# Three pairs of maxima tiles beside each imaginary row's chain, and those rows split and summed by ScalarE and GpSimd

## The chip, the cores and the metric

The kernel runs on one core of a Trainium2 chip. The core has five engines that work beside each other, each through its own instructions in order: TensorE (PE in the profile, with its weight loads as PEld), VectorE (DVE), ScalarE (ACT), GpSimd (POOL) and SyncE (SP), which here issues nearly all DMA transfers. PSUM, into which PE writes, has eight banks of 128 x 512 float32. GpSimd doesn't touch PSUM in this kernel. The metric is the time of one execution on the device in microseconds.

## The reference

Two mixers run on the same `x` (2048 x 512, float32) and are blended by a gate per row:

```python
g = _sigmoid((x * gate_w).sum(-1, keepdims=True))
a = x @ dft_hid_re.T ;  b = x @ dft_hid_im.T          # Fourier mixing along the hidden dimension
A = dft_seq_re @ a - dft_seq_im @ b                    # and along the sequence, real part
q, k, v = heads of x @ wqkv                            # 32 heads of 16
B = concat(softmax(q @ k.T / 4) @ v) @ wo
out = g * A + (1 - g) * B
```

(These lines are shortened from the reference; shapes are written out in it.) The weights of the attention are large (drawn x 64), so the softmax needs its row maxima, and float32 accuracy is kept by splitting operands.

## The kernel before, in words

**Split operands.** Where full accuracy is needed, a float32 tile is written as a high part (a cast to `float32r`) and a low part (the tile minus the high part). `hi_lo` (L73) does it: the cast on ScalarE, the subtraction on VectorE or on the engine that it is given. A product is then three matmuls (`mm3`, L77: high x high, high x low, low x high). A chain of four such triples over the hidden dimension, twelve matmuls, makes one 128 x 512 row tile.

**The order of the work.** The order on every engine is that of the program text (`manual_schedule`). It has these stages:

1. Projections to q and k (L156 to L172), stored split in DRAM (`qk_d`).
2. Value rows (L255 to L264): for each of 16 row tiles `s` a chain into a psS bank, copied to `vt` by ScalarE and VectorE.
3. Imaginary rows (L276 to L297): for each of 16 row tiles a chain with the imaginary part of the hidden matrix into a psS bank; the result is split into `bt` (`hi_lo`, L284) and stored to `b_d` by SP. In the same turn of the loop the row's product with the gate's weight is summed into a column of `z` (L289), the `xa` row for two turns later is loaded, and, for `s` = 2 to 5, a part of the output weight `wo` is split (cast on ScalarE, subtraction on GpSimd) and stored; its next part is loaded only after that store. For `s` = 6 to 9 a part of the real hidden matrix (`wre`) is split in the same way (`split(1)`). The pool of `bt` and `wt` tiles, `hl`, has two buffers; raw loads have six.
4. The main stage (from L768): the gate's values from `z` (`gate`, L603), then the real rows (`real`, L343, copied out of PSUM by ScalarE as `y` and split by GpSimd), the transform along the sequence (`dft`, L368) and the attention, interleaved on PE by written-out patterns (L705 to L707). The stage opens with six bursts of six real-row matmuls, with scores and maxima tiles between them (L771 to L783).

**Maxima tiles.** The softmax's row maxima come from tiles of their own: `a_tile` (L197) multiplies 48 rows of `qs` and `ks` for one head of a pair into one PSUM bank, and VectorE reduces the bank to one column of `mx`. The tiles of a pair's two heads use different row halves of PE. Each head has 1024 such tiles, and some are done ahead, in `visit` (L243), between the chains of stages 2 and 3: two per head and visit, from the value row 10 on, until `LEAD` = 44 per head are done: 22 visits. When the first 32 per head are there, `m_rows` (L213) transposes the block's maxima and SP writes them into `qs`.

**PSUM.** Three psS banks (`s`: rows and scores), three psA banks (`a`), one psD bank (`d`) and one bank `acc`, which collects the attention's values in the main stage. A visit's four tiles go to the three psA banks and the psD bank.

The lines the change touches most are these:

```python
        hi_lo(bt[:, 0], bt[:, 1], ps)
        nc.sync.dma_start(b_d[s], bt.bitcast(F32))
        if s + 2 < NT:
            xgs[s + 2] = staged(xa[s + 2])
        xg = xgs.pop(s)
        nc.vector.scalar_tensor_tensor(xg, xg, 1.0, gwb, op0=ALU.mult, op1=ALU.mult, accum_out=z[:, s:s + 1])
```

Of the kernel before, what the change touches and what calls it, by code (L numbers as in the profile page):

```python
# [9 lines left out]
F32 = mybir.dt.float32  # L10
F32R = mybir.dt.float32r
AF = mybir.ActivationFunctionType
ALU = mybir.AluOpType
AX = mybir.AxisListType

P = 128
S = 2048
D = 512
# [3 lines left out]
KT = D // P  # L22
NT = S // P
UNITS = NP * 32
LEAD = 44
RAW = 6
PSUM = bass.MemoryType.PSUM
DRAM = bass.MemoryType.DRAM
# [3 lines left out]
def mix_kernel(ctx: ExitStack, tc: tile.TileContext, xa_t, xa, wqkv, w_hid, w_seq, wo, gate_w, out):  # L32
# [5 lines left out]
    nc = tc.nc  # L38
    ctx.enter_context(tc.manual_schedule())

    psS = ctx.enter_context(tc.tile_pool(name="psS", bufs=3, space=PSUM))
    psA = ctx.enter_context(tc.tile_pool(name="psA", bufs=3, space=PSUM))
    psO = ctx.enter_context(tc.tile_pool(name="psO", bufs=1, space=PSUM))
    psD = ctx.enter_context(tc.tile_pool(name="psD", bufs=1, space=PSUM))
# [17 lines left out]
    z = const.tile([P, NT], F32, name="z")  # L62
# [8 lines left out]
    acc = psO.tile([P, 512], F32, name="acc")  # L71

    def hi_lo(hi, lo, src, lo_eng=None):  # L73
        nc.scalar.copy(hi, src)  # L74
        (lo_eng or nc.vector).tensor_tensor(lo, src, hi.bitcast(F32), ALU.subtract)  # L75

    def mm3(ps, sh, sl, mh, ml, first, last):  # L77
        nc.tensor.matmul(ps, sh, mh, start=first, stop=False)  # L78
        nc.tensor.matmul(ps, sh, ml, start=False, stop=False)  # L79
        nc.tensor.matmul(ps, sl, mh, start=False, stop=last)  # L80

    right = tc.tile_pool(name="st1", bufs=1, side="right", reuse_waits="tile")
    st1 = right.__enter__()
# [4 lines left out]
    gwb = st1.tile([P, D], F32, name="gwb")  # L88
# [3 lines left out]
    def staged(src):  # L92
        raw = st1.tile([P, D], F32, name="raw", bufs=RAW)
        nc.sync.dma_start(raw, src)
        return raw
# [9 lines left out]
    def split(n):  # L105

        for _ in range(n):
            load_ahead()
            if loaded:
                hi, lo, raw, lo_eng, shape = loaded.pop(0)  # L110
                hi_lo(hi, lo, raw.rearrange("p (s t) -> p s t", s=4) if shape else raw, lo_eng)
            load_ahead()
# [7 lines left out]
    def bank():  # L120
        nonlocal banks
        banks += 1
        return (psS if banks % 2 else psA).tile([P, 512], F32, name="s" if banks % 2 else "a")


    with tc.tile_pool(name="qk", bufs=1, reuse_waits="tile") as pool:
# [29 lines left out]
        for tb in range(4):  # L156
            for c in range(2):
# [9 lines left out]
                for ct in range(4):  # L167
                    ps = bank()
# [28 lines left out]
    def a_tile(i, h, ps=None):  # L197
        p, j = divmod(i, 64)
        qt, kb = divmod(j, 4)
        if ps is None:  # L200
            ps = psA.tile([P, 512], F32, name="a")
        r = slice(64 * h, 64 * h + 48)
        nc.tensor.matmul(ps, qs[p % 2][r, qt * P:(qt + 1) * P], ks[p % 2][r, kb * 512:(kb + 1) * 512],  # L203
                         start=True, stop=True)
        user = nc.vector.tensor_reduce(mx[p % 2][:, h, qt, kb:kb + 1], ps, AX.X, ALU.max)  # L205
        hf = j // 32
        a_left[p, hf] = a_left.get((p, hf), 64) - 1
        if not a_left[p, hf]:
            nc.vector.tensor_reduce(nm[hf], mx[p % 2][:, :, 8 * hf:8 * hf + 8, :], AX.X, ALU.max, negate=True)
            deferred.append((p, hf))  # L210
        return user
# [14 lines left out]
    def run_deferred():  # L226
        while deferred:
            m_rows(*deferred.pop(0))
# [12 lines left out]
    a_next = 0  # L241

    def visit(i):  # L243

        nonlocal a_next
        if i < 10 or a_next == LEAD:
            return
        if a_next % 32 >= 4:
            run_deferred()
        for j in range(2):  # L250
            for h in range(2):
                a_tile(a_next, h, psD.tile([P, 512], F32, name="d") if j and h else None)
            a_next += 1

    for s in range(NT):  # L255
        t = xab[s // 4][:, s % 4]
        ps = psS.tile([P, 512], F32, name="s")
        for kt in range(KT):
            r = slice(kt * P, (kt + 1) * P)
            mm3(ps, t[:, 0, r], t[:, 1, r], wv[0][kt], wv[1][kt], kt == 0, kt == KT - 1)  # L260
        visit(s)
        pv = ps.rearrange("p (r h d) -> p r h d", h=2, d=DH)
        nc.scalar.copy(vt[:, s, :, 0:16], pv[:, :, 0])
        nc.vector.tensor_copy(vt[:, s, :, 17:33], pv[:, :, 1])  # L264
# [11 lines left out]
    for s in range(NT):  # L276
        t = ab[s]
        ps = psS.tile([P, 512], F32, name="s")
        for kt in range(KT):
            r = slice(kt * P, (kt + 1) * P)  # L280
            mm3(ps, t[:, 0, r], t[:, 1, r], wch[:, kt], wcl[:, kt], kt == 0, kt == KT - 1)
        visit(NT + s)
        bt = st1.tile([P, 2, D], F32R, name="hl", bufs=2)
        hi_lo(bt[:, 0], bt[:, 1], ps)  # L284
        nc.sync.dma_start(b_d[s], bt.bitcast(F32))
        if s + 2 < NT:
            xgs[s + 2] = staged(xa[s + 2])
        xg = xgs.pop(s)
        nc.vector.scalar_tensor_tensor(xg, xg, 1.0, gwb, op0=ALU.mult, op1=ALU.mult, accum_out=z[:, s:s + 1])  # L289
        if 2 <= s < 2 + KT:  # L290
            wt = st1.tile([P, 2, D], F32R, name="hl", bufs=2)
            hi_lo(wt[:, 0], wt[:, 1], wos.pop(0), nc.gpsimd)
            nc.sync.dma_start(wo_d[s - 2], wt.bitcast(F32))
            if s + 1 < 2 + KT:
                wos.append(staged(wo[:, s - 1]))
        elif s >= 2 + KT:
            split(1)  # L297
    run_deferred()
    assert a_next == LEAD
    right.__exit__(None, None, None)  # L300
# [547 lines left out]
```

## Time and profile before

| what | value |
|---|---|
| median of 3 runs | 1778.67 us (1777.91 to 1779.57) |
| profiled execution | 1778.45 us, its span 1776.3 us |
| PE / VectorE / ScalarE / GpSimd busy | 98% / 78% / 64% / 19% of the span |
| 128 x 512 maximum out of PSUM, VectorE | 682 ns |
| 128 x 512 copy out of PSUM, ScalarE (`y`) | 581 ns |
| 128 x 512 subtraction, GpSimd / VectorE (`hl`) | 1283 / 687 ns |
| value rows | 95 to 144 us |
| imaginary rows | 144 to 216 us |

In the profile, a group of instructions is written as line, engine, operation, written tile `<-` read tile; then the busy time, the mean duration of one in ns, and the engine's idle time just before them with what ended it. In the timeline the first two numbers are the start and the length in us of a run of equal instructions (`x3`: three of them), and the bracket has the wait before it. Slices are fortieths of the span, their digits tenths of busy time; PEclk is the clock that PE was granted, in tenths of full speed.

### The profile page before, as it was taken

The page shows a single profiled execution, that of the slowest core. Times are in us where ns is not written, and L with a number is a line of the kernel's source. Part 1 is how long each engine was busy: PE and PEld are TensorE (multiplying, and loading weights), DVE is VectorE, ACT ScalarE, POOL GpSimd, SP SyncE. Part 2 cuts the span into 40 slices and gives each one's busy share as a digit, 9 for nine tenths or more (in the row PEclk, how much of TensorE's full clock was granted, in tenths as well). Part 3 has the DMA queues.
Part 4 walks back from the last instruction along what each step waited for, and adds up shares of the span by engine and source line. Part 5 has one row for each costly group of instructions (what it writes and reads, how often), then busy time and mean ns, then how long its engine had stood idle before and what let it go on. Part 6 is the DMA issues. An engine that isn't in the chain of part 4 may idle for free.

```text
span 1776.3 us, 32641 instructions
## 1 busy us (share of the span) xinstructions
PE 1747.2 (98%) x12753; PEld 1044.3 (59%) x12753; DVE 1392.9 (78%) x2347; ACT 1144.5 (64%) x2242; POOL 342.8 (19%) x353
## 2 busy tenths in 40 slices
PE   8999899999999999999999999999999999999997
PEld 7876554456665665665656655665665666544443
DVE  5228878888888888888888888888888888899943
ACT  5211267777677676776776666666666676677775
POOL 0111121221222232221221232221222222100011
PEclk9999899999999999999999999999999999999998
DMA  8754610314132242414146434313142535460113
GB/s 283 238 108 159 216 24 7 55 31 73 43 67 61 58 108 83 90 37 78 43 78 243 92 99 105 80 51 72 48 79 67 122 90 96 156 157 22 38 28 123
DMA packets 77994, 164.71 MB, mean 93 GB/s; under 512 B 14592, under 2 KB 15616, under 8 KB 74000
## 3 DMA queue, kind: packets, MB, share of 16 engines
q1 hardware_dynamic: 77584, 162.56, 36.0%
q8 instruction: 100, 1.64, 0.4%
q14 instruction: 54, 0.44, 0.1%
q0 software_dynamic: 256, 0.07, 0.0%
HBM read 107.47 MB, written 54.52 MB: 91 GB/s over the span
## 4 chain that ended last, share of the span: by engine, by line
PE 89%; DVE 6%; ACT 2%; DMA 1%; issue 1%; DVEq 0%; SPq 0%; ACTq 0%
PE d L339 33%; PE acc L630 25%; PE a L203 11%; PE s L621 11%; DVE mx L205 5%; PE s L78 2%; PE s L79 2%; PE s L80 2%; ACT pt L622 1%; PE a L79 1%; PE a L80 1%; PE a L78 1%; DVE y L396 1%; DMA b<-hl 1%; PE a L339 0%
## 5 line engine op out<-in xcount | busy, mean ns | idle before, releaser
L205 DVE TENSOR_REDUCE mx<-a 128x1 f32<-128x512 f32 x2026 | 1248.1, 682 | 237.7 <-PE a L203 221.3
L622 ACT ACTIVATE pt<-s 128x512 f32<-128x512 f32 x2008 | 1026.1, 622 | 424.5 <-PE s L621 360.1
L203 PE MATMUL a<-ks,qs 48*128 48x512 f32 x2026 | 817.1, 420 | 4.2 <-DVE mx L205 2.4
L621 PE MATMUL s<-qs,ks 50*128 50x512 f32 x2008 | 769.9, 413 | 0.4 <-ACT pt L622 0.2
L339 PE MATMUL d<-xab,ch 64*128 64x512 f32 x2016 | 649.0, 396 | 3.6 <-DVE mx L205 3.6
L630 PE MATMUL acc<-pt,vt 128*17 128x512 f32 x4096 | 506.1, 597 | 0.0
L339 PEld LDWEIGHTS d<-xab,ch 64*128 64x128 f32 x2016 | 365.7, 184 | 128.4 <-DVE mx L205 66.3
L621 PEld LDWEIGHTS s<-qs,ks 50*128 50x128 f32 x2008 | 366.7, 185 | 110.0 <-ACT pt L622 29.8
L203 PEld LDWEIGHTS a<-ks,qs 48*128 48x128 f32 x2026 | 367.0, 185 | 87.6 <-DVE mx L205 58.5
L339 PE MATMUL d<-xab,cl 64*128 64x512 f32 x1008 | 399.7, 396 | 0.0
L323 POOL CAST ch<-craw 128x512 fp32r<-128x512 f32 x126 | 76.9, 611 | 829.7 <-PE d L339 334.1
L339 PEld LDWEIGHTS d<-xab,cl 64*128 64x128 f32 x1008 | 185.5, 184 | 63.7 <-DVE mx L205 47.6
L630 PEld LDWEIGHTS acc<-pt,vt 128*17 128x17 f32 x4096 | 87.8, 96 | 194.0 <-issue 191.2
L324 POOL TENSOR_TENSOR cl<-craw,ch 128x512 fp32r<-128x512 f32 x126 | 162.2, 1288 | 10.1
L339 PE MATMUL d<-wre,xab 64*128 64x512 f32 (+1 forms) x348 | 96.5, 410 | 5.0 <-ACT pt L622 2.5
L339 PEld LDWEIGHTS d<-wre,xab 64*128 64x128 f32 (+1 forms) x348 | 60.7, 187 | 40.2 <-issue 23.5
L339 PE MATMUL d<-wo_hl,o_hl 64*128 64x512 f32 (+1 forms) x261 | 70.9, 397 | 0.0
L339 PEld LDWEIGHTS d<-wo_hl,o_hl 64*128 64x128 f32 (+1 forms) x261 | 47.0, 185 | 13.9 <-issue 9.5
L74 ACT CAST hl<-s 128x512 fp32r<-128x512 f32 x32 | 18.7, 585 | 55.6 <-PE s L80 45.0
L75 DVE TENSOR_TENSOR hl<-s,hl 128x512 fp32r<-128x512 f32 x32 | 22.0, 687 | 31.8 <-ACT hl L74 31.8
L356 POOL CAST xab<-y 128x512 fp32r<-128x512 f32 x16 | 9.8, 611 | 164.7 <-ACT y L355 131.7
L634 ACT COPY oe<-acc 128x512 f32<-128x512 f32 x31 | 18.2, 587 | 32.0 <-PE acc L630 32.0
(123 smaller groups left out, 897.1 us busy)
## 6 DMA issues: line engine op xcount, KB each, us to landing
craw<-w_seq SPq DMA_DIRECT2D x128, 256.0 KB
qk<-hl SPq DMA_DIRECT2D x32, 512.0 KB
qs<-qk SPq DMA_DIRECT2D x96, 128.0 KB
ks<-qk SPq DMA_DIRECT2D x96, 128.0 KB
b<-hl SPq DMA_DIRECT2D x16, 512.0 KB
xab<-b SPq DMA_DIRECT2D x16, 512.0 KB
o<-oe SPq DMA_DIRECT2D x62, 128.0 KB
oh<-nh SPq DMA_DIRECT2D x12, 512.0 KB
```

The costliest lines, as they stand in the source:

```text
L75: (lo_eng or nc.vector).tensor_tensor(lo, src, hi.bitcast(F32), ALU.subtract)
L78: nc.tensor.matmul(ps, sh, mh, start=first, stop=False)
L79: nc.tensor.matmul(ps, sh, ml, start=False, stop=False)
L80: nc.tensor.matmul(ps, sl, mh, start=False, stop=last)
L203: nc.tensor.matmul(ps, qs[p % 2][r, qt * P:(qt + 1) * P], ks[p % 2][r, kb * 512:(kb + 1) * 512], start=True, stop=True)
L205: user = nc.vector.tensor_reduce(mx[p % 2][:, h, qt, kb:kb + 1], ps, AX.X, ALU.max)
L323: nc.gpsimd.tensor_copy(h1, raw)
L324: nc.gpsimd.tensor_tensor(l1, raw, h1.bitcast(F32), ALU.subtract)
L339: i = nc.tensor.matmul(self.ps, st[r], mv[r], start=not self.begun, stop=stop)
L621: nc.tensor.matmul(ps, ks[p % 2][rr, kt * P:(kt + 1) * P], qs[p % 2][rr, q0:q0 + 512], start=True, stop=True)
L622: return nc.scalar.activation(pts[u][:, 2 * qb + h], ps, AF.Exp, bias=0.0, scale=DH ** -0.5)
L630: nc.tensor.matmul(acc[32 * j:32 * j + 17], vt[:, kt, p, 16 * h:16 * h + 17], pt[:, j], start=kt == 0, stop=kt == NT - 1)
```

## The change

`visit` does nothing in the value rows any more (`i < NT`). In the imaginary rows, fifteen visits (after the chains 0 to 14) do three tiles per head each, 45 per head in all instead of 44. The two further tiles of a visit go to the bank `acc` and to a psS bank. The imaginary row is copied by ScalarE from PSUM to a new float32 tile `bf` (two buffers), and GpSimd makes both parts of `bt` from it. The gate's product is done by GpSimd, and its sum over the row by ScalarE, as an activation `Copy` with an accumulator. VectorE has neither of them any more.

```diff
-LEAD = 44
+LEAD = 45
...
-        if i < 10 or a_next == LEAD:
+        if i < NT or a_next == LEAD:
             return
         if a_next % 32 >= 4:
             run_deferred()
-        for j in range(2):
+        for j in range(3):
             for h in range(2):
-                a_tile(a_next, h, psD.tile([P, 512], F32, name="d") if j and h else None)
+
+                ps = (None, None, None, psD, acc, psS)[2 * j + h]
+                if ps in (psD, psS):
+                    ps = ps.tile([P, 512], F32, name="d" if ps is psD else "s")
+                a_tile(a_next, h, ps)
             a_next += 1
...
         visit(NT + s)
+
+        bf = st1.tile([P, D], F32, name="bf", bufs=2)
+        nc.scalar.copy(bf, ps)
         bt = st1.tile([P, 2, D], F32R, name="hl", bufs=2)
-        hi_lo(bt[:, 0], bt[:, 1], ps)
+        nc.gpsimd.tensor_copy(bt[:, 0], bf)
+        nc.gpsimd.tensor_tensor(bt[:, 1], bf, bt[:, 0].bitcast(F32), ALU.subtract)
         nc.sync.dma_start(b_d[s], bt.bitcast(F32))
         if s + 2 < NT:
             xgs[s + 2] = staged(xa[s + 2])
         xg = xgs.pop(s)
-        nc.vector.scalar_tensor_tensor(xg, xg, 1.0, gwb, op0=ALU.mult, op1=ALU.mult, accum_out=z[:, s:s + 1])
+        nc.gpsimd.tensor_tensor(xg, xg, gwb, ALU.mult)
+        nc.scalar.activation(xg, xg, AF.Copy, accum_out=z[:, s:s + 1])
```

## The prediction

> **What bounds the kernel now.** I read the page's shares and slices first, then the stretch that the diff touches (0 to 235 us) by timeline, waits and groups. From the page, engines and slices:
>
> ```profile
> PE 1747.2 (98%) x12753; PEld 1044.3 (59%) x12753; DVE 1392.9 (78%) x2347; ACT 1144.5 (64%) x2242; POOL 342.8 (19%) x353
> ...
> PE   8999899999999999999999999999999999999997
> ...
> PEclk9999899999999999999999999999999999999998
> ```
>
> PE is never short of work except at the start, in the fifth slice (178 to 222 us) and at the end. So a change made before 222 us is worth what it moves the point at which the main stage starts to flow. That point is the third burst of six real-row matmuls (L339), which starts at 221.88, just after ScalarE's first copy `y` (L355, 221.24).
>
> The value rows run from 95.0. A chain of twelve matmuls alone takes 2.73 us; with a visit behind it 3.61. The first imaginary-row chain starts at 144.00. Timeline there, VectorE:
>
> ```profile
> 151.18 1.89 DVE L205 TENSOR_REDUCE mx<-a 128x1 f32<-128x512 f32 x3
> 152.98 0.68 DVE L205 TENSOR_REDUCE mx<-d 128x1 f32<-128x512 f32 x1
> 153.58 0.68 DVE L75 TENSOR_TENSOR hl<-s,hl 128x512 fp32r<-128x512 f32 x1
> 154.18 0.68 DVE L289 SCALAR_TENSOR_TENSOR raw<-raw,gwb 128x512 f32<-128x512 f32 x1
> ```
>
> Six operations at a pitch of 0.60 fill the 3.65 us from one visit to the next: VectorE is full, and PE (2.79 + 0.86) just as much. Then ScalarE gets stuck, in the next view (its timeline):
>
> ```profile
> 165.78 0.59 ACT L74 CAST hl<-s 128x512 fp32r<-128x512 f32 x1 [0.92 <-PE a L203]
> 170.35 0.62 ACT L74 CAST hl<-raw 128x512 fp32r<-128x512 f32 x1 [3.98 <-DMA raw<-wo]
> 171.60 0.59 ACT L74 CAST hl<-s 128x512 fp32r<-128x512 f32 x1 [0.64 <-DMA b<-hl]
> 176.52 0.62 ACT L74 CAST hl<-raw 128x512 fp32r<-128x512 f32 x1 [4.33 <-DMA raw<-wo]
> ```
>
> In visits with an output-weight part (s = 2 to 5) the part's load arrives late, the next row's cast stands behind it on ScalarE, VectorE's subtraction behind that, the maxima behind that. Visits take 4.3 to 6.8 us, about 10 us lost. So this stage has two bounds: VectorE's own work, and a loop through ScalarE and DMA. What the new operations will cost is in the groups by shape:
>
> ```profile
> L357 POOL TENSOR_TENSOR xab<-y,xab 128x512 fp32r<-128x512 f32 x16 | 20.5, 1283 | 1.3
> L472 POOL TENSOR_TENSOR no<-no 128x512 f32<-128x512 f32 x12 | 15.4, 1286 | 20.0 <-DMA no<-r 20.0
> ...
> L356 POOL CAST xab<-y 128x512 fp32r<-128x512 f32 x16 | 9.8, 611 | 164.7 <-ACT y L355 131.7 <-PE a L203 33.0
> ```
>
> **The change, part by part.** The profiled execution took 1778.45 us (span 1776.3 and 2.15 around it), 0.2 below the median of the runs shown; the sum is made against 1778.45.
>
> *Six visits leave the value rows:* 6 x (3.61 - 2.73) = -5.3. Nothing else in that stage is longer than 2.73 (ScalarE 0.38, VectorE 0.42 per chain), so the first imaginary chain starts at 138.7.
>
> *A third pair of tiles per visit:* on PE one pair costs 0.235 (tiles at 209.03 and 209.38 are one and a half pairs apart), so a visit's period is 3.65 + 0.23 = 3.88. VectorE: six maxima at 0.60 = 3.6, and nothing else. Both fit in 3.9. The new PSUM places (`acc`, unused until the first values, and a third of psS) cost nothing by themselves, but the visit's last tile now takes the psS buffer of the row chain before, so PE can run about one and a half rows ahead of ScalarE's copy.
>
> *The rows and the gate on ScalarE and GpSimd.* Here I find the new bound. On GpSimd stand, per row, cast, subtraction and product: 0.70 + 1.35 + 1.29 = 3.34 (durations above; pitch 0.70 and 1.35 from the pair at 222, and from two subtractions in 2.64). ScalarE's sum with accumulator waits for that product, and **the next row's copy `bf` is queued behind the sum on ScalarE**; GpSimd's next cast waits for that copy. The two engines run in turn, not beside each other. One turn: sum 0.65, copy 0.59, hand-over 0.06 (221.83 to 221.89), GpSimd 3.34, hand-over 0.06 = **4.70**, above PE's 3.88.
>
> The sum's duration is not in the trace. Lower end 0.52, the pitch of plain activations (two in 1.09); upper end 0.98, an activation with a vector scale, 0.77 (L393), and a short one for the read-out, 0.21 (L605). VectorE's read-out cost 0.08, so I take 0.65, the row nearest to it; over 15 turns the ends are -2 and +5.
>
> For s = 2 to 9 ScalarE also casts a weight part (0.62) after the sum, and GpSimd subtracts it (1.35) ahead of the next cast: 0.65 + 0.62 + 0.07 + 1.35 + 3.34 + 0.06 = **6.09**.
>
> On top come the loads. For s = 2 to 5 the weight loop is: cast 0.62, subtraction 1.36, SP's store and load issues 0.4, landing 3.7 to 4.2 (166.62 to 170.35, 160.06 to 164.24) = 6.1 to 6.6. The store loop of buffer `hl`: landing 4.5 (167.14 to 171.60), cast 0.70, subtraction 1.29 = 6.5. I take 6.4 for four turns; ends 6.1 (hidden) and 7.5 (waits one behind another, as in the 6.8 of now). At s = 6 the four real-part loads are issued behind that row's store and land 4.8 after the subtraction (179.40 to 184.21); the cast could start at 2.1, so 2.7 is added; lower end 0.
>
> GpSimd's two-input operation took 1.75 once, at 157.92, while VectorE did a product of two SBUF operands; the other rows are 1.27 to 1.32. I take 1.29, since the change leaves VectorE only maxima out of PSUM there. At 1.75 thirty operations would add 14. The Trainium skill (GPSIMD Engine Reference, Specifications) says that GpSimd shares its SBUF interface with VectorE and that they collide when VectorE has two SBUF inputs. By that rule nothing collides after the change, so its sum is mine; by the slow row it would be 14 more.
>
> Chain 0 ends at 141.65; its copy, GpSimd's three and the hand-overs put the first sum at 145.75. Then 2 x 4.70 + 4 x 6.4 + (6.09 + 2.7) + 3 x 6.09 + 5 x 4.70 = 85.6, so the sixteenth sum starts at **231.35**. Today the corresponding VectorE sum ends at 216.92.
>
> *The start of the main stage.* ScalarE: sum 0.65, the gate's exponential (0.25), two exponentials at 0.51, then the copy `y` at 233.3 instead of 221.24: **+12.1**. PE will have done both first bursts by then and waits; VectorE's maxima stand behind the gate's small operations (to about 233). Today's wait of 2.44 for a maximum ahead of the first burst goes, but it is late no more. After today's wait the granted clock was 0.50 from 216 to 219.3; the longer wait (some 6 us) puts the same dip on the third burst and what follows: +1.5, half of 3.3 being lost; ends 0 and 3.
>
> *One tile per head less in the main stage:* -0.25, one pair; ends 0 and -0.5. Row maxima for the first block come up at the same count (36), under the slower loop: nothing. SP's stores wait for GpSimd instead of VectorE, the row loads behind them are two rows ahead: nothing while turns last over 4 us, else the load's landing of about 4.
>
> Sum: 1778.45 + 12.1 + 1.5 - 0.25 = **1791.8**, 0.75% slower.
>
> **The rivals.**
>
> *PE sets the pace (faster).* Where: ScalarE between sum and next copy. If the turn took under 3.9, because GpSimd's product or the sum didn't hold the next copy back, the stage would last 16 x 2.79 + 15 x 1.09 = 61.0 from 138.7, and the first burst start at 200 instead of 215.86: 1763. For it: VectorE is full now and would be free, the maxima no longer stand behind the weights' loads. Against it: both engines work in order, and every row of GpSimd is 1.27 or more. It decides at an average turn of 5.71 - 13.3/15 = 4.8.
>
> *The clock falls inside the stage (slower still).* After a wait of 1.17 at 180.63 matmuls of 0.23 pitch ran at 0.43, with 0.50 granted until 188. With turns of 6.1 to 6.4 PE waits about 2 us in each. At half clock a visit takes 5.1 + 1.7 = 6.8, over eight visits some 5 more than the turn, and up to 10 more if it stays so to s = 15: 1797 to 1807. Against: PE is ahead by more than one row, and a PE that has caught up has no waits. The Trainium skill (TensorE: Matmul & The Clock Gate, Why this matters for your kernels) lets the clock fall only after gaps of some 3 us; the row above fell after less, and the measurement decides. By its rule this rival would be nothing; the sum without it stands.
>
> *The late end is hidden (same).* PE still has the real rows' matmuls and could make up for waiting: 1778. Against: they need ScalarE's copy of each row (PE waits 0.45 and 0.50 us for `y` at 221.88 and 226.52 already), and the main stage shows no idle PE in which to catch up.
>
> **How the numbers follow.** Forecast case 0.70 (1784 to 1799: all low ends -2 -1.2 -2.7 -1.5 -0.25 and most of the high ones), PE's pace 0.09, falling clock or slow GpSimd 0.14, hidden 0.07. Range 1782 to 1803: it leaves out the first rival, the hidden end and a part of the second. What a measurement of this kernel tells from no change is about 0.2% (3.6 us). Faster 0.09; same 0.07; slower 0.84.
>
> **What would show it.** First imaginary chain near 138.7. ScalarE rows of the sum with "POOL raw" as releaser, GpSimd's casts released by "ACT bf", in turns of about 4.7 (plain) and 6.1 to 6.5 (s = 2 to 9); GpSimd busy over 70% from 142 to 231. VectorE idle, PE waiting for `bf` in the psS tile of the visits. The gate's exponential near 232. Wrong if turns are under 4.8 on average, if the copy of a row doesn't wait for the sum before it, or if PE is busy throughout.

## The result, and the profile after

The changed kernel takes 1788.22 us (median of 5 runs, 1786.14 to 1789.95), the kernel before 1779.57 us (5 runs, 1777.91 to 1782.27). The ratio over the runs is 1.0046, 95% interval 1.0035 to 1.0057 (the medians alone would give 1.0049): slower by 0.46%, where 0.75% was forecast and 1782 to 1803 us was the range.

The traced execution of the changed kernel took 1789.95 us (span 1788.1), 11.5 us more than the traced one of before (1778.45), while the medians are 8.65 apart: one trace lies at the upper end of its runs, the other near the lower end of its own. Times inside the stage are compared by the traces below, verdicts by the ratios.

The page's shares and slices after:

```profile
PE 1749.0 (98%) x12753; PEld 1047.3 (59%) x12753; DVE 1373.0 (77%) x2299; ACT 1154.2 (65%) x2274; POOL 391.8 (22%) x401
...
PE   8999889999999999999999999999999999999997
...
PEclk9999899999999999999999999999999999999998
```

PE's slices differ by one digit, in the sixth (223 to 268 us). From 300 to 1700 us PE is busy 1393.33 us before and 1393.43 after: the main stage is nearly the same, and the loss is in the imaginary rows. ScalarE's timeline at two plain rows, and at s = 6 and 7:

```profile
145.04 0.63 ACT L298 ACTIVATE raw<-raw 128x512 f32<-128x512 f32 x1 [3.32 <-POOL raw L297]
145.58 0.19 ACT L298 ACTIVATION_READ_ACCUMULATOR raw<-raw 128x1 f32 x1
145.67 0.57 ACT L289 COPY bf<-s 128x512 f32<-128x512 f32 x1
149.56 0.63 ACT L298 ACTIVATE raw<-raw 128x512 f32<-128x512 f32 x1 [3.32 <-POOL raw L297]
...
178.85 0.63 ACT L298 ACTIVATE raw<-raw 128x512 f32<-128x512 f32 x1 [4.07 <-POOL raw L297]
179.38 0.18 ACT L298 ACTIVATION_READ_ACCUMULATOR raw<-raw 128x1 f32 x1
183.28 0.62 ACT L74 CAST wre<-raw 128x512 fp32r<-128x512 f32 x1 [3.71 <-DMA raw<-w_hid]
183.80 0.58 ACT L289 COPY bf<-s 128x512 f32<-128x512 f32 x1
188.41 0.63 ACT L298 ACTIVATE raw<-raw 128x512 f32<-128x512 f32 x1 [4.03 <-POOL raw L297]
```

And GpSimd's between the two plain sums:

```profile
146.30 0.61 POOL L291 CAST hl<-bf 128x512 fp32r<-128x512 f32 x1 [1.29 <-ACT bf L289]
146.99 1.29 POOL L292 TENSOR_TENSOR hl<-bf,hl 128x512 fp32r<-128x512 f32 x1
148.24 1.29 POOL L297 TENSOR_TENSOR raw<-raw,gwb 128x512 f32<-128x512 f32 x1
```

Read in order of time, this is one chain that goes back and forth: sum (145.04), next row's copy (145.67), cast (146.30), subtraction, product, next sum (149.56), 4.52 us from sum to sum. Each engine waits while the other works. The waits of the stretch from 136 to 245 us say the same:

```profile
ACT raw L298 <- POOL raw L297: 59.0, 16, 4.1
POOL hl L291 <- ACT bf L289: 44.9, 8, 35.9
...
ACT bf L289 <- PE s L80: 2.4, 1, 2.4
```

ScalarE waited for the product in all sixteen rows, and for PE's chain once, at the first row. After that PE was never what a copy waited for. At the end of the stage PE stands (its timeline from 219 us):

```profile
219.34 1.53 PE L348 MATMUL d<-wre,xab 128*128 128x512 f32 x6
...
221.46 1.65 PE L348 MATMUL d<-wre,xab 128*128 128x512 f32 x6
225.02 0.49 PE L630 MATMUL s<-qs,ks 50*128 50x512 f32 x1 [1.91 <-ACT bf L289]
229.74 0.79 PE L630 MATMUL s<-qs,ks 50*128 50x512 f32 x1 [4.23 <-ACT pt L631]
...
231.35 2.93 PE L348 MATMUL d<-wre,xab 128*128 128x512 f32 x6
...
235.10 1.65 PE L348 MATMUL d<-wre,xab 128*128 128x512 f32 x6
```

In the kernel before, the third burst reads:

```profile
221.88 1.66 PE L339 MATMUL d<-wre,xab 128*128 128x512 f32 x6
```

So it starts at 231.35 instead of 221.88, and takes 2.93 instead of 1.66. At the fourth burst (224.14 before) the shift is 10.9, and up to 1200 us it stays between 10.7 and 11.1; by 1705 us it has come down to 10.1.

### The profile page after: what moved, and what is told of

The parts are those of the page before. It is cut to its first block, busy times and chain, and to the rows that moved or that the text cites. A ratio compares the mean times of both kernels' runs of the same rounds, so it can differ in the third digit from the quotient of the medians.

```text
span 1788.1 us, 32639 instructions
## 1 busy us (share of the span) xinstructions
PE 1749.0 (98%) x12753; PEld 1047.3 (59%) x12753; DVE 1373.0 (77%) x2299; ACT 1154.2 (65%) x2274; POOL 391.8 (22%) x401
## 4 chain that ended last, share of the span: by engine, by line
PE 87%; DVE 5%; POOL 3%; ACT 2%; issue 1%; DMA 1%; SPq 0%; DVEq 0%; POOLq 0%; ACTq 0%
PE d L348 33%; PE acc L639 25%; PE s L630 11%; PE a L203 11%; DVE mx L205 4%; PE s L79 2%; PE s L78 2%; PE s L80 2%; ACT pt L631 1%; POOL hl L292 1%; POOL raw L297 1%; PE a L79 1%; PE a L80 1%; PE a L78 1%; DMA raw<-wo 1%
## 5 line engine op out<-in xcount | busy, mean ns | idle before, releaser
L205 DVE TENSOR_REDUCE mx<-a 128x1 f32<-128x512 f32 x2003 | 1233.2, 681 | 253.4 <-PE a L203 237.2
L333 POOL TENSOR_TENSOR cl<-craw,ch 128x512 fp32r<-128x512 f32 x126 | 162.2, 1287 | 10.1
L298 ACT ACTIVATE raw<-raw 128x512 f32<-128x512 f32 x16 | 10.1, 631 | 59.0 <-POOL raw L297 59.0
L268 DVE COPY vt<-s 128x256 f32<-128x256 f32 x16 | 6.8, 424 | 36.3 <-ACT vt L267 36.3
```

Of the source, the lines that this page charges most:

```text
L333: nc.gpsimd.tensor_tensor(l1, raw, h1.bitcast(F32), ALU.subtract)
```

## The experiments

**The rows and the gate alone (e1), the visits alone (e2).** e1 is the kernel before with the new lines for rows and gate, e2 the changed kernel with the old ones:

```diff
-        hi_lo(bt[:, 0], bt[:, 1], ps)
+        bf = st1.tile([P, D], F32, name="bf", bufs=2)
+        nc.scalar.copy(bf, ps)
...
+        nc.gpsimd.tensor_copy(bt[:, 0], bf)
+        nc.gpsimd.tensor_tensor(bt[:, 1], bf, bt[:, 0].bitcast(F32), ALU.subtract)
...
-        nc.vector.scalar_tensor_tensor(xg, xg, 1.0, gwb, op0=ALU.mult, op1=ALU.mult, accum_out=z[:, s:s + 1])
+        nc.gpsimd.tensor_tensor(xg, xg, gwb, ALU.mult)
+        nc.scalar.activation(xg, xg, AF.Copy, accum_out=z[:, s:s + 1])
```

That is e1's edit of the kernel before; e2 is the reverse edit of the changed kernel, whose visits stay.

> Before's 22 visits of two tiles per head, with the changed rows and gate (ScalarE copy, GpSimd split and product, ScalarE sum). Theory (the turn of ScalarE and GpSimd sets the stage's pace, 4.51 us plain and 5.8 to 6.4 with a weight part, whatever the visits are): turns as in the changed kernel, but begun at 144.0 instead of 138.1, so 5.9 us slower than the changed kernel: 1794 us, range 1791 to 1797. Rival (the third pair of tiles in each visit, or the PSUM banks it takes, is what holds the stage): at most the time of before, 1779 us.

Measured: 1796.19 us, the kernel before beside it 1781.08; ratio 1.0084 (1.0070 to 1.0097). The turns are the changed kernel's, plain ones at 4.52 (from 151.60 to 156.11 and 160.64), and the third burst starts at 238.34, 7.0 later than in the changed kernel (5.9 was expected; the first sum is 6.6 later, and the turn at s = 6 took 9.90 instead of 9.56). The theory's number holds, the rival's doesn't: without the third pair of tiles the turns are as long, and the stage ends later because it begins later.

> The fifteen visits of three tiles per head, with before's rows and gate (ScalarE cast, VectorE subtraction and gate sum). Theory: no turn of ScalarE and GpSimd; VectorE is the bound with six maxima, subtraction and gate sum, 6 x 0.60 + 0.60 + 0.66 = 4.86 us a visit, and the visits with an output-weight part stay at 6.2 to 6.8: third burst of real rows near 226 instead of 221.9, 1783 us, range 1779 to 1787. Rival (the visits cost nothing, only the moved rows and gate do): 1779 - 5 = 1774 us or less.

Measured: 1781.99 us, ratio 1.0002 (0.9993 to 1.0010): no difference. By its absolute time that lies in the theory's range, by its ratio between theory and rival: the visits neither gain nor lose. The trace shows both halves. The stage begins at 138, as in the changed kernel, but VectorE's plain turns are 4.80 (146.25, 151.04, 155.84), the third burst starts at 228.54 (226 was expected), and ScalarE's lines show the old stall, longer:

```profile
176.69 0.62 ACT L74 CAST hl<-raw 128x512 fp32r<-128x512 f32 x1 [5.90 <-DMA raw<-wo]
177.93 0.59 ACT L74 CAST hl<-s 128x512 fp32r<-128x512 f32 x1 [0.63 <-DMA b<-hl]
186.02 0.62 ACT L74 CAST wre<-raw 128x512 fp32r<-128x512 f32 x1 [7.51 <-DMA raw<-w_hid]
```

So the two halves of the change are +0.84% and 0, and together +0.46%: the visits give the stage an earlier start (5.9 us), which a stage at ScalarE's and GpSimd's pace can use, and one at VectorE's pace spends on the further maxima and the longer stalls.

**The order on ScalarE (e3), and on GpSimd (e5).** In e3 the sum is issued one row late, from a tile of its own:

```diff
         nc.scalar.copy(bf, ps)
+        if s:
+            nc.scalar.activation(pg, pg, AF.Copy, accum_out=z[:, s - 1:s])
...
-        nc.gpsimd.tensor_tensor(xg, xg, gwb, ALU.mult)
-        nc.scalar.activation(xg, xg, AF.Copy, accum_out=z[:, s:s + 1])
+        pg = st1.tile([P, D], F32, name="pg", bufs=2)
+        nc.gpsimd.tensor_tensor(pg, xg, gwb, ALU.mult)
+        if s == NT - 1:
+            nc.scalar.activation(pg, pg, AF.Copy, accum_out=z[:, s:s + 1])
```

> The changed kernel with ScalarE's sum of a row's gate product issued after the copy of the next row (the product goes to a tile of its own). Theory: the next row's copy no longer stands behind the product, plain rows go at PE's 3.9 us, rows with real-part weights at GpSimd's own 4.5, rows with output weights at 6.2 by their loads: 9 us less than the changed kernel, 1779 us, range 1776 to 1783. Rival (the loads and PE's clock set the pace, the order on ScalarE does not): 1788 us, unchanged.

Measured: 1775.93 us, ratio 0.9964 (0.9951 to 0.9978). The same work on the same engines, with the sum one place later, turns a loss of 0.46% into a gain of 0.36%. This is the experiment that decides for the order on ScalarE: the plain copies come at 3.89 and 3.94 (141.57, 145.46, 149.40), PE's pace, and PE's chain is what they wait for:

```profile
145.46 0.59 ACT L289 COPY bf<-s 128x512 f32<-128x512 f32 x1 [3.30 <-PE s L80]
...
149.40 0.59 ACT L289 COPY bf<-s 128x512 f32<-128x512 f32 x1 [2.74 <-PE s L80]
```

The gain is larger than expected: 9 us were forecast, the third burst starts 13.0 earlier than in the changed kernel (218.31), and the time lies just under the range. Behind the late loads at s = 6 the next copy follows after 1.61 us (181.24, 182.85), since PE's row was ready, and the three after it at 4.61, 4.04 and 3.88, where 4.5 was expected.

In e5 the product moves ahead on GpSimd, and the sum stays where it was on ScalarE:

```diff
         nc.scalar.copy(bf, ps)
         bt = st1.tile([P, 2, D], F32R, name="hl", bufs=2)
+        xg = xgs.pop(s)
+        nc.gpsimd.tensor_tensor(xg, xg, gwb, ALU.mult)
+        nc.scalar.activation(xg, xg, AF.Copy, accum_out=z[:, s:s + 1])
         nc.gpsimd.tensor_copy(bt[:, 0], bf)
...
-        xg = xgs.pop(s)
-        nc.gpsimd.tensor_tensor(xg, xg, gwb, ALU.mult)
-        nc.scalar.activation(xg, xg, AF.Copy, accum_out=z[:, s:s + 1])
```

> The changed kernel with one thing moved: GpSimd makes the gate's product, which needs nothing of the row's chain, ahead of the row's cast and subtraction. Theory (the next copy stands behind the sum, the sum behind the product, the product behind cast and subtraction): the sum finds its product ready, the copies go at PE's 3.9 us where no weight part is, and the last sum ends with the last copy; only the loads' waits (turns of 6.3 for s = 2 to 5, one of some 8 at s = 6) stay. Third burst near 215, 16 us earlier than in the changed kernel; 1773 us, range 1769 to 1777. Rival (GpSimd's work as such is the bound): unchanged, 1788 us.

Measured: 1776.18 us, before 1780.77; ratio 0.9973 (0.9962 to 0.9983). The time is in the range, but the third burst starts at 218.93, not at 215. ScalarE's timeline at s = 8 to 10:

```profile
188.75 0.63 ACT L293 ACTIVATE raw<-raw 128x512 f32<-128x512 f32 x1 [2.67 <-POOL raw L292]
...
193.18 0.63 ACT L293 ACTIVATE raw<-raw 128x512 f32<-128x512 f32 x1 [2.70 <-POOL raw L292]
...
197.58 0.63 ACT L293 ACTIVATE raw<-raw 128x512 f32<-128x512 f32 x1 [2.69 <-POOL raw L292]
```

After the late load at s = 6 GpSimd has four instructions, 4.4 us, in each row with a weight part and is never ahead again, so the sums wait for it to the end (the last one, at 215.09, by 2.33), though for 4.4 us and less instead of 5.8 a row. Here GpSimd's work is the bound, which the expectation had left out.

**The weight parts' loads (e4).**

```diff
-    wos = [staged(wo[:, 0])]
+    wos = [staged(wo[:, i]) for i in range(4)]
...
+        if s % 2 and s >= NT - 2 * KT:
+            wt = st1.tile([P, 2, D], F32R, name="hl", bufs=2)
+            hi_lo(wt[:, 0], wt[:, 1], wos.pop(0), nc.gpsimd)
+            nc.sync.dma_start(wo_d[KT - 1 - len(wos)], wt.bitcast(F32))
```

The four lines stand in the loop of the value rows; the old ones go from the imaginary rows.

> The changed kernel with the four output-weight parts split and stored beside the value rows 9, 11, 13, 15, all four loads issued ahead. Theory: four turns of 5.8 to 6.4 become plain turns of 4.51, 6.7 us less: 1781.5 us, range 1779 to 1784; ScalarE still waits for GpSimd's product in every turn. Rival (the late loads are the whole loss, and without them PE sets the pace): 1770 us or less.

Measured: 1784.59 us, ratio 1.0020 (1.0012 to 1.0029); against the changed kernel's 1.0046 a gain of about a quarter of a per cent (each ratio to the runs of before beside it). The rows s = 2 to 5 now turn in 4.49 to 5.37, and ScalarE still waits for GpSimd's product in all sixteen rows. The time is 0.6 us above the range: the four turns gave 5.9 us instead of 6.7, and the turn at s = 6 took 10.09 instead of 9.56. The late loads are a part of the loss and not its cause.

**The gate's sum back on VectorE (e6).**

```diff
-        nc.gpsimd.tensor_tensor(xg, xg, gwb, ALU.mult)
-        nc.scalar.activation(xg, xg, AF.Copy, accum_out=z[:, s:s + 1])
+        nc.vector.scalar_tensor_tensor(xg, xg, 1.0, gwb, op0=ALU.mult, op1=ALU.mult, accum_out=z[:, s:s + 1])
```

> The changed kernel with the gate's product and sum back on VectorE in one instruction; the rows' split stays on ScalarE and GpSimd. Theory: without the sum on ScalarE nothing of GpSimd's stands ahead of the next copy; VectorE has 6 x 0.60 + 0.66 = 4.26 us a visit, which is then the pace of plain rows, and the loads' turns stay: third burst near 217, 1776 us, range 1772 to 1780. Rival (the rows' split on GpSimd is what holds the stage): 1785 us or more.

Measured: 1775.69 us, ratio 0.9968 (0.9957 to 0.9979). The rows' split on GpSimd is not what holds the stage; the sum in ScalarE's queue was the link. The third burst starts at 222.06, not at 217, and nearly all of that shows at one visit, between the copies at 200.34 and 209.38. GpSimd, then VectorE, then PE, in their timelines:

```profile
196.93 1.29 POOL L292 TENSOR_TENSOR hl<-bf,hl 128x512 fp32r<-128x512 f32 x1
...
197.19 1.57 DVE L297 SCALAR_TENSOR_TENSOR raw<-raw,gwb 128x512 f32<-128x512 f32 x1
...
204.06 0.79 PE L203 MATMUL a<-ks,qs 48*128 48x512 f32 x1 [2.94 <-DVE mt L218]
```

VectorE's products took 1.66, 1.57 and 1.20 (at 191.76, 197.19 and 202.29) instead of 0.68 while GpSimd worked; the copies of the first block's row maxima came late behind them, PE stood 2.94 us for them, and its granted clock was 0.50 from 203.9 to 207.3. The long products are not the whole cause: they add 2.4 us, and the visit was 5.2 too long. In e2 GpSimd had nothing to do there and the products took 0.68, and the same visit shows the same wait:

```profile
208.54 0.79 PE L203 MATMUL a<-ks,qs 48*128 48x512 f32 x1 [2.31 <-DVE mt L218]
```

In both kernels VectorE's plain visits take longer than PE's 3.89 (4.20 in e6, by the products from 145.32 to 162.12; 4.80 in e2), so it can be behind when the copies are due. How the 5.2 us divide between the two causes isn't shown.

**Loads early without the change (e7), and both cures on it (e8).** e7 is the kernel before with e4's edit, eight raw buffers, and the real-part weights loaded before the imaginary rows and split at s = 2 to 5; e8 is the changed kernel with that and with e5's edit:

```diff
-RAW = 6
+RAW = 8
...
         add(wre[0][kt], wre[1][kt], w_hid[0, :, kt], nc.gpsimd)
+    load_ahead()
...
-        elif s >= 2 + KT:
+        if 2 <= s < 2 + KT:
             split(1)
```

> The kernel before, with the output-weight parts split beside the value rows 9, 11, 13, 15 and the real-part weights loaded ahead of the imaginary rows and split at s = 2 to 5 (eight raw buffers). Theory: the 10 us that visits lose there to late loads go, VectorE's 3.66 us a visit is the pace throughout: third burst near 212 instead of 221.9, 1770 us, range 1767 to 1774. Rival (DMA bandwidth, not the order, holds those visits): 1777 us or more.

Measured: 1767.23 us, ratio 0.9926 (0.9911 to 0.9941). The visits keep 3.65 us almost throughout, the third burst starts at 210.21. The 10 us that visits lost before the change were the order of loads and splits, not DMA bandwidth.

> The changed kernel with both cures: product ahead of cast and subtraction, and the weight parts' loads and splits moved as in the run on the kernel before. Theory: nothing holds a copy any more, PE sets the pace at 3.89 us a visit from 138: third burst near 204, 18 us earlier than before the change, 1762 us, range 1759 to 1768. This is the time of the first rival of the prediction (PE sets the pace). Rival (GpSimd's 4.5 us in rows with a weight part, or the gate's end, take the place): 1768 to 1772 us.

Measured: 1762.55 us, ratio 0.9897 (0.9880 to 0.9914): 1% faster than before, 1.5% faster than the change as it was. The third burst starts at 207.52 (204 was expected). ScalarE's timeline at two late rows, and PE's:

```profile
190.90 0.59 ACT L294 COPY bf<-s 128x512 f32<-128x512 f32 x1 [1.66 <-PE s L80]
192.20 0.63 ACT L298 ACTIVATE raw<-raw 128x512 f32<-128x512 f32 x1 [0.71 <-POOL raw L297]
195.44 0.59 ACT L294 COPY bf<-s 128x512 f32<-128x512 f32 x1 [2.51 <-PE s L80]
...
207.52 1.66 PE L347 MATMUL d<-wre,xab 128*128 128x512 f32 x6
```

Now the copies wait for PE's chains, as they should: PE sets the pace, and the burst takes 1.66 at a granted clock of 1.00: from 139 to 207 us PE's longest wait is 0.65. The 3.5 us that it is later than expected lie with the first copy (142.43, where the changed kernel has 141.14), with GpSimd in rows with a weight part (sums at 153.30, 157.72, 162.13, 166.54, each 0.5 over PE's 3.89) and with the row of the block's maxima (copies at 190.90 and 195.44).

## Why the prediction was right

The mechanism was the one forecast, in its place: ScalarE's sum waits for GpSimd's product, the next row's copy stands behind the sum, GpSimd's cast behind the copy. e3, e5 and e6 each cut one link of it, and each brought the time from above that of the kernel before to below it. By the terms of the sum:

| term | forecast | trace after |
|---|---|---|
| first imaginary chain | 138.7 | 138.14 |
| first sum starts | 145.75 | 145.04 |
| plain turn, seven | 4.70 each | 4.46 to 4.52, 31.5 in all |
| turns with output-weight parts, four | 6.4 each | 5.81, 6.34, 6.23, 6.39 |
| turn at s = 6 (late real-part loads) | 8.79 | 9.56 |
| turns with real-part weights, three | 6.09 each | 5.79, 5.77, 5.78 |
| sixteenth sum starts | 231.35 | 228.24 |
| first copy `y`, against 221.24 before | +12.1 | +8.8 (230.06) |
| slow clock at the third burst | +1.5 | +2.1 (10.9 - 8.8) |
| one tile per head less | -0.25 | shift from 10.9 at the fourth burst to 10.1 at 1705 us, of which the tile's part is not shown |
| slow clock at 1716 us | not in the sum | +1.5 |
| together | +13.3 | +11.5 by the traced executions, +8.65 by the medians |

The direction and the range held; the size was 13.3 against 8.65. The term that was mis-sized is the turn, 0.2 us too long in plain rows and 0.3 in rows with a weight part. GpSimd's two-input instructions follow each other at 1.25 (146.99 to 148.24), shorter than one lasts, where 1.35 was read off two subtractions in 2.64; and the accumulator's read-out (0.19) lies mostly beside the activation, so the sum costs ScalarE 0.63. The fifteen turns took 83.2 us instead of 85.6, and the first sum came 0.7 earlier: 3.1 of the 3.3 us by which the copy `y` came before its forecast. One turn was too short in the sum: at s = 6 the loads landed 5.7 after the row's subtraction (177.57 to 183.28), where 4.8 was taken. GpSimd's two-input time stayed at 1.26 to 1.30, as taken, and not at the 1.75 of the other bound. Of the signs, two were missed in size: GpSimd was busy 67% from 142 to 231 us, not over 70%, and the gate's exponential stands at 228.99, not near 232.

The traced executions differ by 2.85 us more than the medians. Of this 1.5 can come from one place, late in the main stage: nine matmuls with `wo_hl` at 1715.62 took 3.83 us at a granted clock of 0.50, where the trace of before has 2.33 at 1.00 (1705.52). The traces of e3 and e8 show the same (3.91 and 3.90), those of the other six experiments 2.32 to 2.36, so it isn't particular to the changed kernel. The rest I can't place: the runs of the kernel before spread over 4 us beside the changed kernel and over 7.5 beside the first experiments (1777.36 to 1784.86, with granted clocks of 0.996 and 0.991), and each trace is one run.

The rivals: *PE sets the pace* was a good number for another kernel. Its 1763 is what e8 took (1762.55), once the sum no longer held the copies and the loads were ahead. That the two agree so closely is in part luck: e8's first burst starts at 202.96 and not at 200, and the kernel before took 1780.77 beside it. *The clock falls inside the stage* happened without deciding anything. After a wait of 1.87 us, which ended at 168.46, the granted clock was 0.50 from 169.9 to 173.2; around one of 5.21, which ended at 184.43, from 183.6 to 190.3; and after one of 1.05 at 195.97 from 197.2 to 200.5. But PE was ahead by more than a row, as argued, and no copy waited for it. The Trainium skill (TensorE: Matmul & The Clock Gate, Why this matters for your kernels) names idle gaps of some 3 us as the point from which the clock falls; the 1.87 and the 1.05 here disagree, and the measurement decides. *The late end is hidden* did not happen: of the shift of 10.9 at the fourth burst 10.1 are still there at 1705 us, and the span is 11.8 longer.

## What to carry to other kernels

Moving work to idle engines is priced by the chain of waits through them, not by their busy share: GpSimd was 22% busy over the span and ScalarE 65%, and together they slowed the kernel, since each waited for the other once per row. Write the loop of one turn with each engine's order, and let no instruction that waits for the slow engine stand ahead of the one that feeds it; work that needs nothing of the chain (here the gate's product) goes first. Then look for the same fault in what was there already: casts queued behind late loads had cost the kernel before 0.7%, more than the whole change moved.

## What the runs showed of the hardware

A VectorE instruction with two SBUF inputs and a GpSimd subtraction get in each other's way, and in these rows the one that starts second pays. Before the change VectorE's product started at 157.84 and took its 0.68, and GpSimd's subtraction, from 157.92, took 1.75 instead of 1.29. In e6 GpSimd's subtraction started at 196.93 and took its 1.29, and VectorE's product, from 197.19, took 1.57 instead of 0.68; the products at 191.76 (1.66) and 202.29 (1.20) also started inside a GpSimd subtraction, from 191.58 and 201.68. The changed kernel, where VectorE only reduces from PSUM in this stage, shows neither. This agrees with what the Trainium skill (GPSIMD Engine Reference, Specifications) says of the shared SBUF interface; that VectorE can be the one that stretches, by up to 1.0 us, was not expected here.
